# Attention and two feed-forward blocks on one core: the last tile of the spatial product stacked, P V issued ahead of the spread of the inverse sums, dense work given out by rows

## The chip, the cores and the metric

The kernel runs on one core of a Trainium2 chip. Its time is the device time of one execution in microseconds (us), the median of three runs. Where the text speaks of a profiled execution, that is one more execution, recorded instruction by instruction.

## What is computed

Three blocks follow one another on four batches (B = 4) of 576 tokens with 8 heads of 64, so a model width of 512:

```python
scores = scale * q @ k.T                       # per head, 576 x 576
kth = np.partition(scores, -32, axis=-1)[..., -32:-31]
attn = softmax(np.where(scores >= kth, scores, -1e9))
x = attn @ v                                   # heads side by side: B x 576 x 512

xk, xr = mix(x, x_prev, mu_k), mix(x, x_prev, mu_r)
x2 = sigmoid(xr @ w_r) * (relu(xk @ w_k) ** 2 @ w_v)

h = gelu(x2 @ w_in)                            # 1024 columns: u, v
v_n = layernorm(v) * g_ln
v_s = einsum('ts,bsd->btd', w_sg, v_n) + b_sg  # over the 576 tokens
out = x2 + (u * v_s) @ w_out
```

The product with `w_sg`, which runs over the tokens, is called the spatial product here. The weights come as 64-bit floats.

## The kernel before

**Precision.** Products of the dense part work on numbers split into a high and a low part (`split`, line 96: ScalarE copies the high part, GpSimd, or VectorE in the tail, subtracts for the low one). Each product is three passes that add up in PSUM, high by high, low by high and high by low (`PASSES`, line 468: the first index is the part of the activation, the second that of the weight). The weights are converted and split once (`conv`) and kept in scratch in DRAM (`ws_r`, `ws_k`, `ws_v`, `ws_sg`, `ws_h`, `ws_u`, `ws_o`), from which `wload` brings them tile by tile into six buffers `w`.

**Attention.** The work is cut in 80 slots. A slot is 128 rows of queries for two heads (`t.hs` = 2, 256 rows of scores) or, for the last 64 queries of a pair, those of both heads in one tile (`t.hs` = 1, a half slot). Batch 0 goes through its pairs twice, for two slots and then three; the others have five slots for each of four pairs, the fifth a half slot. The slots of one pair that are worked off together are a unit: `u.ch` = 0 has two slots, `u.ch` = 1 has three, the last a half slot. For each slot `emit_S` makes the scores on TensorE, two slots ahead; `emit_topk` finds the 32nd largest value of each row on VectorE (max, match_replace and a last scalar_tensor_tensor that masks the exponentials E and sums them, line 308); `emit_T` transposes E on TensorE into `PT` and, for the 64 last keys, `PTr`. At the end of a unit `emit_unit` (line 337) copies the sums on ScalarE (line 342), inverts them on VectorE (343), spreads them over partitions with small products against the identity (348, and 354 for the half slot; called the spread), copies that to `rb` (357), makes P V in PSUM (`px`; 361 over four tiles of 128 keys, 365 for the last 64), and multiplies both into x (372, 376).

**Dense work.** When a batch's attention is done, `part1` (mixing, lines 499 to 508; the r, k and v products; the product with `w_in`; gelu; layernorm, `norm`) and `part2` (the spatial product `E`, lines 697 to 717, and the output product `F`, 724 to 741) of that batch are cut into items and queued in `Dense`. The loop over the slots runs items until a quota is used up (line 833: the work that is left, divided by the slots up to the next batch); items have a priority five slots later than the slot that gives them out. The part of the last batch runs when all slots are done; this is called the tail.

**Spatial product.** There are eight items `E` for each batch, one for each of four column tiles of v_n and each half (288) of the output tokens. An item sums over five token tiles of v_n: four of 128 rows and one of 64, each in three passes, 15 matmuls in one PSUM bank. Afterwards the result is scaled and biased (711 or 714), multiplied with u and split into `gt`. An item `F` takes 12 matmuls over `gt` and `w_out`.

**Order.** A scheduler orders each engine's instructions by these priorities and by its own estimates. What it makes is fixed: each engine takes its instructions strictly in that order. All DMAs here are issued by SyncE, in order too.

## Time and profile before

| | us |
|---|---|
| median of 3 runs | 1044.78 |
| lowest, highest | 1043.91, 1047.49 |
| profiled execution | 1042.54 |
| its span | 1040.8 |

| engine | busy, us | share of the span |
|---|---|---|
| TensorE matmuls (PE) | 896.8 | 86% |
| TensorE weight loads (PEld) | 766.4 | 74% |
| VectorE (DVE) | 888.0 | 85% |
| ScalarE (ACT) | 716.5 | 69% |
| GpSimd (POOL) | 509.7 | 49% |

In the rows further down, the slices cut the span in 40 pieces of 26 us; each digit is the busy share in tenths. A stage row has the start and end, its length, then for each engine the busy time and the number of instructions, then TensorE's granted clock as a share of full speed, the busy share of the DMA engines and their GB/s. A group row has the line, engine, operation, output and inputs, shapes and count, then the busy time in us and the mean in ns, then the idle time ahead of these instructions and what ended it. A timeline row has the start, the duration, engine, line, operation and count, and in brackets the idle time of that engine just before and its releaser ("issue" is a wait that no recorded event explains). A row of the chain of work that ended last has start, duration, engine, output, line and count. A transfer row ends with the size and the median time from issue to landing. Matmuls overlap, so their durations in a row are longer than their spacing. An fp32 product shows as two records.

### The profile page before, as it was taken

How to read it: one execution, taken by the hardware profiler on the slowest of the kernel's cores; microseconds unless marked ns; L12 is line 12 of the kernel's file. 1: busy time of each engine (PE TensorE's matmuls, PEld its weight loads, DVE VectorE, ACT ScalarE, POOL GpSimd, SP SyncE). 2: the span in 40 equal slices, each digit the busy share in tenths (PEclk: the TensorE clock that was granted, in tenths of full speed). 3: DMA queues.
4: the chain of work that ended last, by engine and by line, in shares of the span. 5: the costliest groups of instructions: out<-in, count | busy, mean ns of one | idle time of the engine just before them, and what ended most of it. 6: DMA issues, size and time to landing. Idle time of an engine off the chain costs nothing.

```text
span 1040.8 us, 18998 instructions
## 1 busy us (share of the span) xinstructions
PE 896.8 (86%) x6158; PEld 766.4 (74%) x6158; DVE 888.0 (85%) x2509; ACT 716.5 (69%) x1591; POOL 509.7 (49%) x624
## 2 busy tenths in 40 slices
PE   3542656689989998977999999998999999999997
PEld 2432444469868987866988887777998888799895
DVE  5999899999989999999999999999999998812142
ACT  6866876877598769666786688667786696554340
POOL 6877676745276317766733217389242135310051
PEclk9965665779989999988999999999999999999999
DMA  7674873567745653541333443254333434765431
GB/s 207 221 256 154 271 254 123 179 229 246 236 174 181 198 176 114 165 159 28 130 112 97 138 120 90 73 173 166 107 130 98 135 87 137 285 240 150 117 98 65
DMA packets 103406, 164.36 MB, mean 158 GB/s; under 512 B 19201, under 2 KB 72961, under 8 KB 103297
## 3 DMA queue, kind: packets, MB, share of 16 engines
q1 hardware_dynamic: 103296, 163.05, 48.4%
q8 instruction: 51, 0.84, 0.3%
q14 instruction: 59, 0.48, 0.1%
HBM read 133.09 MB, written 29.92 MB: 157 GB/s over the span
## 4 chain that ended last, share of the span: by engine, by line
PE 43%; DVE 25%; ACT 9%; POOL 5%; issue 3%; DMA 2%; SPq 0%; DVEq 0%; POOLq 0%; ACTq 0%
PE d L515 7%; PE d L580 7%; DVE M L281 6%; DVE T L287 5%; DVE E L308 5%; PE d L704 4%; PE tp L361 4%; PE d L625 3%; DVE T L273 3%; PE tp L515 2%; PE S L238 2%; DVE T L272 2%; PE d L732 2%; PE tp L321 2%; DVE M L292 2%
## 5 line engine op out<-in xcount | busy, mean ns | idle before, releaser
L281 DVE MAX8 M<-T 128x8 f32<-128x288 f32 x576 | 237.7, 444 | 1.4
L287 DVE MATCH_REPLACE8 T<-M,T 128x288 f32<-128x288 f32 x432 | 187.6, 439 | 0.0
L515 PE MATMUL d<-xm,w 128*128 128x288 f32 (+2 forms) x1008 | 159.6, 308 | 8.6 <-POOL xm L100 4.9
L515 PEld LDWEIGHTS d<-xm,w 128*128 128x128 f32 x1008 | 143.4, 196 | 11.5 <-POOL xm L100 5.8
L238 PE MATMUL S<-kst,qst 128*128 128x288 f32 x512 | 114.5, 342 | 43.1 <-ACT qst L200 26.1
L308 DVE SCALAR_TENSOR_TENSOR E<-S,kth,E 128x576 f32<-128x576 f32 x144 | 146.0, 1045 | 1.4 <-ACT kst L213 0.5
L321 PE MATMUL tp<-ident,E 128*128 128x128 f32 x512 | 87.0, 308 | 48.9 <-ACT kst L207 21.2
L238 PEld LDWEIGHTS S<-kst,qst 128*128 128x128 f32 x512 | 85.0, 213 | 53.3 <-ACT qst L200 27.2
L321 PEld LDWEIGHTS tp<-ident,E 128*128 128x128 f32 x512 | 67.7, 158 | 57.2 <-ACT kst L207 22.2
L307 ACT ACTIVATE E<-S,nb 128x576 f32<-128x576 f32 x144 | 104.9, 770 | 1.2
L580 PE MATMUL d<-ksq,w 128*128 128x288 f32 (+2 forms) x672 | 101.4, 300 | 0.0
L240 ACT ACTIVATE S<-S 128x576 f32<-128x576 f32 x128 | 83.2, 650 | 23.4 <-PE S L238 22.2
L580 PEld LDWEIGHTS d<-ksq,w 128*128 128x128 f32 x672 | 91.6, 188 | 0.7 <-issue 0.6
L322 ACT ACTIVATE PT<-tp 128x512 f32<-128x512 f32 x128 | 73.7, 598 | 19.6 <-PE tp L321 19.4
L273 DVE TENSOR_TENSOR T<-S 128x576 f32<-128x576 f32 (+1 forms) x80 | 81.1, 1014 | 0.0
L272 DVE TENSOR_TENSOR T<-S 128x576 f32<-128x576 f32 (+1 forms) x81 | 69.6, 859 | 9.4 <-ACT S L240 9.3
L704 PE MATMUL d<-w,vn 128*128 128x288 f32 (+1 forms) x420 | 71.8, 310 | 0.5 <-DMA w<-ws_sg 0.5
L361 PE MATMUL tp<-PT,rawv 128*64 128x256 f32 (+1 forms) x512 | 71.7, 424 | 0.0
L100 POOL TENSOR_TENSOR ksq<-tmp,ksq 128x576 fp32r<-128x576 f32 (+2 forms) x32 | 40.3, 1260 | 54.3 <-ACT ksq L98 54.2
L704 PEld LDWEIGHTS d<-w,vn 128*128 128x128 f32 (+1 forms) x420 | 58.4, 187 | 10.0 <-issue 7.8
L100 POOL TENSOR_TENSOR splk<-rawk,splk 128x256 fp32r<-128x256 f32 x40 | 33.2, 831 | 62.5 <-ACT splk L98 52.7
L292 DVE MAX8 M<-T 128x8 f32<-128x288 f32 x144 | 58.5, 440 | 0.0
(162 smaller groups left out, 2010.5 us busy)
## 6 DMA issues: line engine op xcount, KB each, us to landing
w<-ws_k SPq DMA_DIRECT2D x40, 512.0 KB, 4.2
w<-ws_v SPq DMA_DIRECT2D x40, 512.0 KB, 4.4
w<-ws_r SPq DMA_DIRECT2D x20, 512.0 KB, 4.6
w<-ws_h SPq DMA_DIRECT2D x20, 512.0 KB, 3.8
w<-ws_u SPq DMA_DIRECT2D x20, 512.0 KB, 4.1
w<-ws_sg SPq DMA_DIRECT2D x32, 288.0 KB, 3.3
w<-ws_o SPq DMA_DIRECT2D x16, 512.0 KB, 4.8
rawk<-in_k_dram SPq DMA_DIRECT2D x40, 128.0 KB, 3.0
```

What stands on the lines that cost most here:

```text
L238: nc.tensor.matmul(ps[:, hf, :HALF], lhsT=su.qst[h, t.u.ch][:, a, 128 * t.i:128 * t.i + 128], rhs=su.kst[h][:, HALF * hf:HALF * hf + HALF] ...
L272: nc.vector.tensor_tensor(T[:, h, :HALF], t.S[:, h, :HALF], t.S[:, h, HALF:], op=OP.max)
L273: nc.vector.tensor_tensor(T[:, :, HALF:], t.S[:, :, :HALF], t.S[:, :, HALF:], op=OP.min)
L281: nc.vector.max(M[:, h, 8 * r:8 * r + 8], src[h])
L287: nc.vector.match_replace(L[h], M[:, h, 8 * r:8 * r + 8], src[h], NEG)
L307: nc.scalar.activation(E, Sx, AF.Exp, bias=nb[:, h:h + 1], scale=0.125)
L308: nc.vector.scalar_tensor_tensor(E, Sx, kv[h], E, op0=OP.is_ge, op1=OP.mult, accum_out=u.sums[:, c + h:c + h + 1])
L321: nc.tensor.transpose(ps[:, kc, :], E[:, h, 64 * h + 128 * kc:64 * h + 128 * kc + 128], ident)
L361: nc.tensor.matmul(px[64 * h:64 * h + 64, :n], lhsT=vr[:, 4 * h + kc, :], rhs=u.PT[h][:, kc, :n], start=(kc == 0), stop=False)
L515: nc.tensor.matmul(ps[:, :n_], lhsT=w[:, bb, 128 * c:128 * c + 128], rhs=act[ch, which, c][:, a, o:o + n_], start=(c == 0 and i == 0), sto ...
L580: nc.tensor.matmul(ps[:, :nn], lhsT=w[:, bb, 128 * (f % 4):128 * (f % 4) + 128], rhs=kt[f][:, a, o:o + nn], start=(f == 0 and i == 0), sto ...
L704: nc.tensor.matmul(ps[:, :HALF], lhsT=act[b, "vn", i][:nn, a, 128 * m:128 * m + 128], rhs=W["sg", i, si][:nn, bb, :HALF], start=(j == 0), ...
```

## The change

Three edits.

The last token tile of v_n has 64 rows. The change puts its low part into partitions 64 to 127 of the tile's high part (a DMA from SBUF to SBUF behind the split, in `norm`) and keeps the weights of that tile with their high part twice, one above the other, and their low part above zeros (`conv`). One pass of 128 rows then gives high by high plus low by high, and a second gives high by low: an item of the spatial product has 14 matmuls, all of 128 rows. The loads of these weights now bring 128 rows.

In `emit_unit` the P V products over the four full key tiles are written ahead of the spread, and the products over the last 64 keys behind it, alternating with the spread of the half slot; the copy to `rb` comes after both.

The quota of a slot is weighed by its rows (`t.hs`) against the rows of the slots up to the next batch, instead of by the number of slots.

```diff
@@ -341,6 +341,11 @@
         rinv = sb.tile([128, 5], F32, tag="rinv", name="rinv", bufs=2)
         nc.scalar.activation(rinv[:, :nt], u.sums[:, :nt], AF.Copy, bias=1e-9)
         nc.vector.reciprocal(rinv[:, :nt], rinv[:, :nt])
+        px = bank("tp")
+        for kc in range(4):
+            for h in range(2):
+                nc.tensor.matmul(px[64 * h:64 * h + 64, :n], lhsT=vr[:, 4 * h + kc, :], rhs=u.PT[h][:, kc, :n],
+                                 start=(kc == 0), stop=False)
 
         ps = bank("tp")
         for i in range(2):
@@ -348,21 +353,14 @@
                 nc.tensor.matmul(ps[64 * h:64 * h + 64, 128 * i:128 * i + 128],
                                  lhsT=rinv[:, 2 * i + h:2 * i + h + 1].to_broadcast([128, 64]), rhs=ident,
                                  start=True, stop=True)
-        if u.ch:
-            for h in range(2):
-                s = slice(64 * h, 64 * h + 64)
+        for h in range(2):
+            s = slice(64 * h, 64 * h + 64)
+            nc.tensor.matmul(px[s, :n], lhsT=vr[s, 8, :], rhs=u.PTr[s, :n], start=False, stop=True)
+            if u.ch:
                 nc.tensor.matmul(ps[s, 256:320], lhsT=rinv[s, 4:5].to_broadcast([64, 64]), rhs=ident[s, s],
                                  start=True, stop=True)
         rb = sb.tile([128, 320], F32, tag="rb", name="rb", bufs=1)
         nc.scalar.activation(rb[:, :n], ps[:, :n], AF.Copy)
-        px = bank("tp")
-        for kc in range(4):
-            for h in range(2):
-                nc.tensor.matmul(px[64 * h:64 * h + 64, :n], lhsT=vr[:, 4 * h + kc, :], rhs=u.PT[h][:, kc, :n],
-                                 start=(kc == 0), stop=False)
-        for h in range(2):
-            s = slice(64 * h, 64 * h + 64)
-            nc.tensor.matmul(px[s, :n], lhsT=vr[s, 8, :], rhs=u.PTr[s, :n], start=False, stop=True)
         if (b, p) not in xT:
             x = sb.tile([128, S + 1], F32, tag="x", name="x", bufs=5)
             xT[b, p] = x
@@ -424,6 +422,11 @@
                 split(w[:n, 0, :HALF], w[:n, 1, :HALF], nat[:n, HALF * hf:HALF * hf + HALF])
                 scr = dram.tile([128, 2, HALF], F32, name=f"ws_sg{i}_{hf}")
                 nc.sync.dma_start(scr[:n], w[:n, :, :HALF].bitcast(F32))
+                if n == 64:
+
+                    nc.gpsimd.memset(w[64:, 1, :HALF].bitcast(F32), 0.0)
+                    nc.sync.dma_start(scr[64:, 0], w[:64, 0, :HALF].bitcast(F32))
+                    nc.sync.dma_start(scr[64:, 1], w[64:, 1, :HALF].bitcast(F32))
                 wscr["sg", i, hf] = scr
             return
         H, L = raw[:, :, 1], raw[:, :, 0]
@@ -459,9 +462,8 @@
             tag = WTAGS[wturn[0] % len(WTAGS)]
             wturn[0] += 1
         w = sb.tile([128, 2, 512], F32R, tag=tag, name="w", bufs=WBUFS[tag])
-        n = 64 if key[:2] == ("sg", 4) else 128
-        wv = w[:n, :, :HALF] if kind == "sg" else w
-        nc.sync.dma_start(wv.bitcast(F32), wscr[key][:n])
+        wv = w[:, :, :HALF] if kind == "sg" else w
+        nc.sync.dma_start(wv.bitcast(F32), wscr[key])
         return w
 
 
@@ -645,6 +647,9 @@
             nc.gpsimd.tensor_scalar(ag[:nn, 3:4], ag[:nn, 0:1], -1.0, 1.0, op0=OP.mult, op1=OP.mult)
             nc.gpsimd.tensor_scalar(t, y, ag[:nn, 3:4], ag[:nn, 2:3], op0=OP.add, op1=OP.mult)
             split(a[:nn, 0], a[:nn, 1], t)
+            if nn < 128:
+
+                nc.sync.dma_start(a[64:, 0].bitcast(F32), a[:64, 1].bitcast(F32))
             if len(segs) == 2 or i > 1:
                 act[b, "vn", i] = a
             else:
@@ -699,10 +704,9 @@
             ps = bank("d")
             j = 0
             for i in range(5):
-                nn = 128 if i < 4 else 64
-                for a, bb in PASSES:
-                    nc.tensor.matmul(ps[:, :HALF], lhsT=act[b, "vn", i][:nn, a, 128 * m:128 * m + 128],
-                                     rhs=W["sg", i, si][:nn, bb, :HALF], start=(j == 0), stop=(j == 14))
+                for a, bb in (PASSES if i < 4 else ((0, 0), (0, 1))):
+                    nc.tensor.matmul(ps[:, :HALF], lhsT=act[b, "vn", i][:, a, 128 * m:128 * m + 128],
+                                     rhs=W["sg", i, si][:, bb, :HALF], start=(j == 0), stop=(j == 13))
                     j += 1
             y = tmp()[:, :HALF]
             if si == 0:
@@ -830,7 +834,7 @@
         if s in ready:
             ready[s]()
         nxt = min([r for r in ready if r > s], default=NS)
-        quota = 0.995 * dense.left() / (nxt - s)
+        quota = 0.995 * dense.left() * t.hs / sum(x.hs for x in slots[s:nxt])
         with at(1000 * (s + 5) + 500):
             while dense.items and quota > 0:
                 quota -= dense.run()
```

How this moves instructions. On TensorE at the end of the last slot, where E_11596 (before) and E_11581 (after) are the masked exponentials of the last, half slot, tp and d are PSUM banks, L732 (L736) is the output product of batch 2 and L704 the spatial product, before:

```order
L704 MATMUL d<-w,vn 128x288 x16
L732 MATMUL d<-w,gt 128x512 x6
L329 MATMUL tp<-ident,E_11596 128x128 x4
L333 MATMUL tp<-ident,E_11596 64x64
L334 MATMUL tp<-ident,E_11596 64x64
L732 MATMUL d<-w,gt 128x512 x3
L348 MATMUL tp<-ident,rinv 64x128 x4
L354 MATMUL tp<-ident,rinv 64x64 x2
L732 MATMUL d<-w,gt 128x512 x9
L361 MATMUL tp<-PT,rawv 64x320 x8
L365 MATMUL tp<-PTr,rawv 64x320 x2
L732 MATMUL d<-w,gt 128x512 x18
```

and after, at the same place:

```order
L736 MATMUL d<-w,gt 128x512 x18
L329 MATMUL tp<-ident,E_11581 128x128 x4
L333 MATMUL tp<-ident,E_11581 64x64
L334 MATMUL tp<-ident,E_11581 64x64
L736 MATMUL d<-w,gt 128x512 x18
L347 MATMUL tp<-PT,rawv 64x320 x8
L353 MATMUL tp<-ident,rinv 64x128 x4
L358 MATMUL tp<-PTr,rawv 64x320
L360 MATMUL tp<-ident,rinv 64x64
L358 MATMUL tp<-PTr,rawv 64x320
L360 MATMUL tp<-ident,rinv 64x64
L736 MATMUL d<-w,gt 128x512 x12
```

Twelve more output matmuls stand ahead of the last slot's transposes, the spread has moved behind P V, and 24 output matmuls follow the unit (the 12 shown and 12 of 64 rows).

On TensorE in the tail, at the start of the last batch's spatial product (vn_12678 before and vn_12663 after are the last token tile, the numbers of d and tp tell the items apart), before:

```order
L704 MATMUL tp_12744<-w_12470,vn_12678 128x288
L704 MATMUL d_12766<-w_12394,vn_12596 128x288 x2
L704 MATMUL d_12766<-w_12422,vn_12624 128x288 x3
L704 MATMUL tp_12744<-w_12470,vn_12678 128x288 x2
L704 MATMUL d_12766<-w_12468,vn_12650 128x288 x3
L704 MATMUL d_12766<-w_12470,vn_12678 128x288 x3
```

and after:

```order
L708 MATMUL d_12751<-w_12453,vn_12635 128x288 x3
L708 MATMUL tp_12772<-w_12333,vn_12555 128x288 x3
L708 MATMUL tp_12772<-w_12379,vn_12581 128x288 x3
L708 MATMUL tp_12772<-w_12407,vn_12609 128x288 x3
L708 MATMUL tp_12772<-w_12453,vn_12635 128x288 x3
L708 MATMUL tp_12730<-w_12455,vn_12663 128x288 x2
L708 MATMUL d_12751<-w_12455,vn_12663 128x288 x2
L708 MATMUL tp_12772<-w_12455,vn_12663 128x288 x2
```

The last tile's matmuls of the first item stood among those of the second; now the full tiles of three items come first, 36 matmuls, and then the last tile of all three.

On VectorE at the end of the top-k part (L714 and L718 are the bias step of the spatial product, L504 and L506 a mix of the next batch, L308 the last step of the last slot), before:

```order
L714 SCALAR_TENSOR_TENSOR tmp_11293<-d_11277,gln_77,bsg_78 128x288
L281 MAX M_11469<-T2_11594 128x8
L295 TENSOR_REDUCE M_11469<-M_11469 128x8
L296 TENSOR_REDUCE kth_11470<-M_11469 128x1
L308 SCALAR_TENSOR_TENSOR E2_11596,sums_11468<-S2_11455,kth_11470,E2_11596 128x576
L714 SCALAR_TENSOR_TENSOR tmp_11314<-d_11298,gln_77,bsg_78 128x288
L504 SCALAR_TENSOR_TENSOR tmp_11671<-x_9191,omu_76,tmp_11671 128x576
```

and after:

```order
L718 SCALAR_TENSOR_TENSOR tmp_11299<-d_11284,gln_77,bsg_78 128x288
L287 MATCH_REPLACE T2_11579<-M_11454,T2_11579 128x288
L281 MAX M_11454<-T2_11579 128x8
L295 TENSOR_REDUCE M_11454<-M_11454 128x8
L296 TENSOR_REDUCE kth_11455<-M_11454 128x1
L506 SCALAR_TENSOR_TENSOR tmp_11656<-x_9168,omu_76,tmp_11656 128x576
L308 SCALAR_TENSOR_TENSOR E2_11581,sums_11453<-S2_11440,kth_11455,E2_11581 128x576
```

The bias step of the batch's last item and one mix have moved ahead of the last top-k step.

## Rows read from the trace of the kernel before

**Rows 1.** Page, 40 equal slices of the span, busy tenths

```profile
PE   3542656689989998977999999998999999999997
...
DVE  5999899999989999999999999999999998812142
```

**Rows 2.** Stages: PE, PEld, DVE, ACT, POOL busy (count), clock, DMA

```profile
400.00:500.00 100.00, 86.30 (x561) 70.94 (x560) 97.74 (x272) 71.85 (x157) 70.51 (x72) 0.91 0.35 113
...
700.00:800.00 100.00, 96.25 (x750) 87.09 (x749) 98.38 (x296) 74.54 (x171) 50.02 (x53) 0.98 0.39 127
...
889.94:1000.57 110.63, 110.63 (x754) 101.58 (x752) 37.25 (x71) 54.56 (x115) 16.28 (x31) 1.00 0.62 202
1000.57:1019.94 19.37, 19.37 (x124) 16.44 (x122) 7.76 (x15) 6.20 (x14) 7.36 (x8) 1.00 0.01 3
```

**Rows 3.** Groups of VectorE instructions between 300 and 890 us

```profile
L714 DVE SCALAR_TENSOR_TENSOR tmp<-d,gln,bsg 128x288 f32<-128x288 f32 x16 | 8.0, 506 | 3.2 <-PE d L704 3.2
L343 DVE RECIPROCAL rinv<-rinv 128x5 f32<-128x5 f32 (+1 forms) x22 | 3.8, 171 | 9.9 <-ACT rinv L342 9.9
```

**Rows 4.** Timeline around the last slot's end, all engines

```profile
888.54 1.38 DVE L308 SCALAR_TENSOR_TENSOR E<-S,kth,E 128x576 f32<-128x576 f32 x1
...
890.29 0.80 DVE L504 SCALAR_TENSOR_TENSOR tmp<-x,omu,tmp 128x576 f32<-128x576 f32 x1
...
894.32 0.42 ACT L357 ACTIVATE rb<-tp 128x320 f32<-128x320 f32 x1
...
898.09 0.19 PEld L365 LDWEIGHTS tp<-PTr,rawv 64*64 64x64 f32 x4 [0.49 <-issue]
...
898.78 3.95 PEld L732 LDWEIGHTS d<-w,gt 128*128 128x128 f32 x18 [0.49 <-issue]
...
898.90 0.42 DVE L372 TENSOR_TENSOR x<-tp,rb 128x256 f32<-128x256 f32 x1 [2.46 <-PE tp L365]
...
902.99 1.23 PE L515 MATMUL tp<-xm,w 128*128 128x288 f32 x8
```

**Rows 5.** Chain of work that ended last, two of its pieces

```profile
943.64 1.58 PE d L515 x12
...
1022.96 2.75 PE d L732 x12
```

**Rows 6.** Timeline of weight loads, one spatial item in the tail

```profile
1010.44 1.61 PEld L704 LDWEIGHTS tp<-w,vn 128*128 128x128 f32 x12 [0.16 <-issue]
1012.22 0.42 PEld L704 LDWEIGHTS tp<-w,vn 64*128 64x128 f32 x3 [0.16 <-issue]
1012.82 1.62 PEld L704 LDWEIGHTS d<-w,vn 128*128 128x128 f32 x12 [0.17 <-ACT gt L98]
```

**Rows 7.** Timeline at the start of the tail's spatial product

```profile
1000.70 1.48 PE L704 MATMUL tp<-w,vn 128*128 128x288 f32 x10
...
1002.64 0.68 DVE L100 TENSOR_TENSOR vn<-tmp,vn 64x512 fp32r<-64x512 f32 x1 [1.18 <-ACT vn L98]
```

**Rows 8.** Transfers of 128 KB: count, size, median us to landing

```profile
rawv<-in_v_dram SPq DMA_DIRECT2D x40, 128.0 KB, 2.3
...
x2sTrue<-xn SPq DMA_DIRECT2D x8, 128.0 KB, 3.0
...
out_dram<-xr SPq DMA_DIRECT2D x4, 128.0 KB, 4.0
```

**Rows 9.** Group of GpSimd instructions, forms kept apart

```profile
L100 POOL TENSOR_TENSOR w<-nat,w 128x288 fp32r<-128x288 f32 x8 | 8.0, 1008 | 1.4 <-ACT w L98 1.4
```

**Rows 10.** Groups of ScalarE table loads, forms kept apart

```profile
L480 ACT ACT_TABLE_LOAD x15 | 19.2, 1283 | 0.3
...
L307 ACT ACT_TABLE_LOAD x14 | 18.0, 1283 | 0.3
```

**Rows 11.** Stages of line 308 on VectorE alone

```profile
400.00:500.00 100.00, 21.78 (x36) 0.91 0.35 113
...
700.00:800.00 100.00, 19.20 (x36) 0.98 0.39 127
```

## Prediction

> **What bounds the kernel now.** I read the slices of the whole span first [rows 1]: VectorE is at eight or nine tenths from the second slice up to about 860 us, and at one to four tenths after about 910 us, where TensorE stays at nine. So there are two parts with different limits. In the stages [rows 2] the top-k part shows VectorE busy 97.74 and 98.38 of 100 us; TensorE is close behind it, but VectorE is the engine that hardly ever waits. From 889.94 to 1019.94 TensorE is busy every microsecond (110.63 of 110.63, then 19.37 of 19.37), at the full granted clock of 1.00, which is the 2.4 GHz level, while VectorE is busy for about a third of the time. The turn between the two parts is the last top-k instruction of the last slot, at 888.54 [rows 4].
>
> This sorts the edits. A TensorE microsecond saved behind the turn is a microsecond of the end. One saved ahead of it counts only where VectorE waits for it. In the list of VectorE groups between 300 and 890 us [rows 3] those waits are few: 9.9 us for the copy of the row sums on ScalarE and 3.2 us for the spatial product are the largest.
>
> **Part 1, the stacked last tile.** Each item of the spatial product takes 15 matmuls: 12 of full height and 3 of 64 rows. The loads show what the short tile costs [rows 6]: 12 loads take 1.61 us, then stand 0.16 us, 3 short loads take 0.42 us, and another 0.17 us passes before the next item; start to start that is 2.38 us. Twelve matmuls of the same 288 columns without a change of height take 1.58 us [rows 5], 0.132 us each, and there the result changes from item to item as well, so the gaps belong to the change of height. Fourteen full matmuls should take 14 x 0.132 = 1.85 us, 0.53 us less. The tail has eight items, which took 19.37 us [rows 2]; 112 matmuls at 0.132 us are 14.8 us, a gain of **4.5 us**. The other 24 items lie in the top-k part and save about as much each, but VectorE hides them.
>
> The Trainium skill ("TensorE: Matmul & The Clock Gate", section "LDWEIGHTS (loading the stationary operand)") says that a load's time follows its columns and not its rows. The rows agree for the load alone (0.42 us for 3, 1.61 us for 12), but they show two gaps more, which that rule doesn't have; by the rule alone the tail's gain would be 8 x 0.132 = 1.1 us.
>
> What it adds: a copy from SBUF to SBUF of 128 KB for each batch, behind the split of the last tile, which the last two matmuls of an item wait for. In the tail the split ends at 1002.64 + 0.68 = 1003.32 [rows 7]. No such copy is in the trace; transfers of 128 KB land between 2.3 and 4.0 us after their issue, those of the same size that start in SBUF and go to a scratch in 3.0 us [rows 8]; so it lands between 1005.6 and 1007.3. By the order, 36 matmuls of three items now stand ahead of the first that needs it: 1000.70 + 36 x 0.132 = 1005.5. TensorE waits between 0.1 and 1.8 us; I take **+0.8 us**, by the 3.0 us, since that transfer too starts in SBUF. Behind it on its queue stand only result stores and reloads of x, which are not wanted before 1020. In the other three batches the copy stands ahead of the second half of the spatial weights on SyncE's queue; a late copy there holds TensorE, and so the scores for a later slot, but these are given out two slots ahead (some 20 us). I cost it at nothing; without that cover it is 3 x 3.0 us. The padded stores and two clears happen once, in the first 200 us; a GpSimd pass over 288 columns takes 1.0 us [rows 9], so they are 2 us on GpSimd at most and nothing on the path.
>
> **Part 2, P V ahead of the spread.** The number of matmuls is the same. In units with a half slot the two 64-row spreads now stand among the 64-row products, so two turns of height become one pair. Such a turn shows 0.49 us on either side of the last products [rows 4]. For the last unit I count **-0.3 us** (bounds 0 and -1.0); the other 15 such units lie under VectorE. The price: the copy of the spread (rb, 0.42 us on ScalarE at 894.32 [rows 4]) ran beside P V before; now it comes behind the unit's last matmul, and x follows it. In the last unit x is then some 1.3 us later than 898.90. That is covered: from x to the first product that needs it took about 4.1 us (898.90 to 902.99 [rows 4]), and by the order 24 matmuls of the output product (24 x 0.23 = 5.5 us, 2.75 us for 12 [rows 5]) and at least nine others now stand there.
>
> **Part 3, dense work by rows.** It changes nothing in the total; I counted the dense matmuls between the transposes of one slot and the next in the order of either kernel. The half slots don't get less: work is given out five slots ahead, and TensorE runs late, so it lands anywhere. What does change is the end: before the last slot's transposes 18 output matmuls now stand instead of 6 (60 in the batch). Those 12 leave the tail: 12 x 0.23 = **-2.75 us**. They cost nothing where they go, since the eight spatial items of this batch just before give back 8 x 0.53 = 4.2 us. On VectorE, however, a bias step (0.5 us) and a mix (0.8 us, as at 890.29) now stand ahead of the last top-k step, and three bias steps in a row wait for items whose matmuls are interleaved. Against that stand the 3.2 us of such waits of before [rows 3], which shrink with the items. The bounds are -2 and +1.3 us; I take **+0.5 us**.
>
> **The top-k part as a whole.** All orders shift, and VectorE's own instructions stay the same in number. ScalarE loses four of its 29 table loads (1.28 us each [rows 10]), and the 9.9 us in which VectorE waited for the copy of the sums stand partly behind such loads. On the other side, the same 36 score steps took 21.78 us in one stage and 19.20 us in another [rows 11], the longer with GpSimd busy 70.51 us and the shorter with 50.02 us [rows 2]: a new neighbourhood can stretch or shorten VectorE by 2 or 3 us in 100 us, mostly cancelling over eight such stages. I take **-1.0 us**, with bounds -6 and +4.
>
> **Sum**, against the profiled execution (1042.54 us, span 1040.8): -4.5 + 0.8 - 0.3 - 2.75 + 0.5 - 1.0 = -7.25, so 1035.3 us. The median of the runs is 2.2 us above the profiled one; carried over, the forecast is 1044.8 - 7.25 = **1037.5 us**.
>
> **Rivals.** (a) The gaps belong to something else, say the turn from one item to the next, and stay; then the stacked tile gives 8 x 0.132 = 1.1 us and not 4.5: 1040.9 us. For it: the second gap does stand at a turn. Against: the first doesn't, and plain items turn without one [rows 5]. This is also what the skill's rule on loads named above would give. Chance 0.10.
> (b) TensorE is nearer to being the bound of the top-k part than VectorE's busy share tells, and the 12.7 us that 24 items save there, with fewer table loads, take away 5 us of the 9.9 + 3.2 us of waits beyond what I counted: 1032.5 us. Chance 0.13.
> (c) The new order puts more GpSimd passes beside VectorE's score steps or makes it wait in-order for dense results, 4 us in all over 890 us: 1041.5 us. Chance 0.12.
> (d) Slower: x now waits for a copy that starts only behind the unit's last product. VectorE takes its work in order, so if the two multiplies of a unit stand too early, it idles in each of 31 units for the copy (0.42 us) and whatever ScalarE has in hand (0.6 us or so). It needs 0.34 us a unit, 10.5 us in all, to bring the kernel to 0.3% slower; 0.45 us a unit gives 1051 us. Against it: the rows show no such wait among the large ones between 300 and 890 us, and the order keeps some 15 VectorE instructions between the reciprocal and the multiplies. Chance 0.07.
>
> **How the numbers follow.** The forecast has 0.58. About 0.3% (3.1 us) is what a measurement of this kernel can tell from no change. Faster by more: nearly all of the forecast (0.56), all of (b), 0.06 of (a) and half of (c), 0.81, which I round to 0.80. Slower by more: most of (d), 0.06. The rest, 0.14, is no change. The range takes in (a), (c) and most of (b): 1031.0 to 1043.5 us.
>
> **What would show it.** In the profile after: items of 14 matmuls at 1.85 us, no 64-row loads in the spatial product, the tail from the last top-k step to the end shorter by some 7 us, one wait of 0.1 to 1.8 us for the copy about three items into the last spatial product, 25 table loads for gelu and exp in place of 29, and the last top-k step within 2 us of 888.5. It is wrong if that step moves by more than 4 us, if VectorE waits for x in many units, or if items still take over 2 us.

## The result and the profile after

| | before | after |
|---|---|---|
| median of 6 runs each, us | 1044.35 | 1029.96 |
| lowest, highest | 1042.97, 1047.49 | 1026.84, 1033.3 |
| profiled execution | 1042.54 | 1030.12 |
| its span | 1040.8 | 1027.9 |
| start of the span to the end of the last top-k step | 889.9 | 882.8 |
| from there to the end | 150.9 | 145.1 |

The ratio is 0.987 (95% interval 0.9847 to 0.9893); the medians are 14.4 us apart, where 7.25 were forecast. 1029.96 lies 1 us under the range. Of the 12.9 us between the spans, 7.0 lie ahead of the last top-k step and 5.9 behind it; the forecast had 0.5 and 6.75. The tail came out about as long as worked out. The top-k part did not.

The slices of the page after, to set beside [rows 1], show the same two parts:

```profile
PE   3652656679989998977999998999999998999996
...
DVE  5999899999999989899999989899999989722142
```

Stages of before (first two lines) and of after (last two), from 260 us to the last top-k step and from there to the end; columns as in [rows 2]:

```profile
260.00:889.86 629.86, 596.73 (x4291) 514.13 (x4290) 598.60 (x1780) 464.68 (x1019) 304.37 (x371) 0.98 0.42 134
889.94:1040.80 150.86, 144.12 (x935) 128.63 (x933) 50.13 (x96) 61.20 (x129) 24.54 (x40) 0.99 0.49 160
```

```profile
260.00:882.82 622.82, 586.02 (x4258) 513.84 (x4258) 592.11 (x1770) 459.81 (x1015) 307.65 (x371) 0.98 0.43 138
882.90:1027.90 145.00, 136.97 (x917) 125.33 (x915) 48.35 (x94) 58.66 (x126) 22.12 (x38) 0.99 0.51 162
```

The first line of before is what the prediction should have printed. Over the whole stretch TensorE is busy 596.73 of 629.86 us and VectorE 598.60: both 95%, each idle for 31 to 33 us. The two stages of [rows 2] had shown 86 and 96 us of 100 for TensorE, and the text called VectorE alone the bound. After the change TensorE has 10.7 us less work in this stretch and VectorE 6.5 us less, though VectorE has 2509 instructions in either kernel. Part of that comes from where the window begins: the last top-k step of batch 0 ends at 262.5 us before and at 259.4 after, so 10 instructions fewer lie in the second window. From that step to the last one the time is 627.5 and 623.4 us. VectorE's busy time in it falls from 596.2 to 592.7 us, and 3.1 of these 3.5 us are in line 308; its idle time falls from 31.3 to 30.7 us. So of the 7.0 us about 3 lie in batch 0, which the prediction did not look at, 3.5 are shorter VectorE instructions, and only 0.6 are shorter waits.

The tail's spatial product in the chain of work of after (start, duration, engine, output, line, count):

```profile
994.19 1.58 PE tp L708 x12
995.77 0.13 issue
995.89 0.50 PE tp L708 x2
996.39 0.26 PE d L708 x2
996.66 0.26 PE tp L708 x2
996.92 1.84 PE d L708 x14
998.77 1.84 PE tp L708 x14
```

and the copy on its queue and the first loads that need it, in the timeline:

```profile
993.49 0.52 SPq L652 DMA_DIRECT2D vn<-vn  x1
...
995.86 0.30 PEld L708 LDWEIGHTS tp<-w,vn 128*128 128x128 f32 x2 [0.33 <-issue]
```

Fourteen matmuls take 1.84 us (forecast 1.85; 2.38 for the 15 of [rows 6]); the copy landed 2.3 us after its issue and was used 2.4 us after it, and TensorE stood 0.33 us for it.

The last slot's end in the timeline of after, to set beside [rows 4]:

```profile
881.53 1.35 DVE L308 SCALAR_TENSOR_TENSOR E<-S,kth,E 128x576 f32<-128x576 f32 x1
...
882.00 2.35 PE L736 MATMUL d<-w,gt 128*128 128x512 f32 x9 [0.99 <-DMA w<-ws_o]
...
884.19 0.60 PE L329 MATMUL tp<-ident,E 128*128 128x128 f32 x4
...
893.14 0.44 ACT L363 ACTIVATE rb<-tp 128x320 f32<-128x320 f32 x1 [6.77 <-PE tp L360]
893.62 0.43 DVE L370 TENSOR_TENSOR x<-tp,rb 128x256 f32<-128x256 f32 x1 [3.35 <-ACT rb L363]
```

Of the 18 output matmuls ahead of the last transposes, nine waited for their weights and ran while the last top-k step was ending; five of them began behind its end. The output product's share of the tail, before (first line) and after, with the busy time and the number of its matmuls and then of its weight loads:

```profile
889.94:1040.80 150.86, 28.50 (x119) 20.26 (x117) 0.99 0.49 160
882.90:1027.90 145.00, 25.68 (x109) 18.47 (x107) 0.99 0.51 162
```

Ten output matmuls have left the tail, 2.8 us of busy time, where the forecast had 12 and 2.75 us.

VectorE's waits of after between 260 and 883 us (us in total, times, longest), beside [rows 3]:

```profile
DVE rinv L343 <- ACT rinv L342: 11.0, 6, 4.0
DVE bst L643 <- ACT vraw L482: 5.1, 3, 3.8
DVE tmp L718 <- PE d L708: 4.0, 3, 2.1
DVE T L272 <- ACT S L240: 2.3, 2, 2.1
DVE x L370 <- ACT rb L363: 1.7, 2, 1.2
```

The wait of x for the copy rb, the mechanism of rival (d), is 1.7 us in two places. The wait for the sums (9.9 us in [rows 3], 11.0 here) did not shrink.

### The profile page after: what moved, and what is told of

Its sections match the earlier page's. It is cut to its first block, busy times and chain, and to the rows that moved or that the text cites. A ratio compares the mean times of both kernels' runs of the same rounds, so it can differ in the third digit from the quotient of the medians.

```text
span 1027.9 us, 18922 instructions
## 1 busy us (share of the span) xinstructions
PE 880.5 (86%) x6126; PEld 767.2 (75%) x6126; DVE 882.6 (86%) x2509; ACT 712.3 (69%) x1587; POOL 514.3 (50%) x626
## 4 chain that ended last, share of the span: by engine, by line
PE 42%; DVE 35%; ACT 10%; POOL 6%; issue 3%; DMA 3%; SPq 1%; DVEq 0%; POOLq 0%; ACTq 0%
DVE M L281 9%; PE d L582 8%; DVE T L287 8%; PE d L517 7%; DVE E L308 6%; PE d L627 4%; DVE T L273 3%; DVE T L272 3%; PE S L238 3%; PE tp L347 3%; PE tp L517 2%; PE d L736 2%; DVE M L292 2%; PE tp L321 2%; PE d L708 2%
## 5 line engine op out<-in xcount | busy, mean ns | idle before, releaser
L281 DVE MAX8 M<-T 128x8 f32<-128x288 f32 x576 | 237.8, 444 | 1.5
L517 PE MATMUL d<-xm,w 128*128 128x288 f32 (+2 forms) x1008 | 154.5, 303 | 8.0 <-DMA w<-ws_k 3.3
L517 PEld LDWEIGHTS d<-xm,w 128*128 128x128 f32 x1008 | 140.6, 192 | 9.9 <-DMA w<-ws_k 3.4
L308 DVE SCALAR_TENSOR_TENSOR E<-S,kth,E 128x576 f32<-128x576 f32 x144 | 143.6, 1028 | 1.1 <-ACT E L307 0.5
L321 PEld LDWEIGHTS tp<-ident,E 128*128 128x128 f32 x512 | 64.7, 156 | 66.1 <-ACT kst L207 26.6
L240 ACT ACTIVATE S<-S 128x576 f32<-128x576 f32 x128 | 83.5, 652 | 19.5 <-PE S L238 18.1
L347 PE MATMUL tp<-PT,rawv 128*64 128x256 f32 (+1 forms) x512 | 83.3, 445 | 1.2 <-ACT PT L322 1.1
L708 PE MATMUL d<-w,vn 128*128 128x288 f32 x392 | 62.4, 309 | 2.8 <-DMA w<-ws_sg 1.7
L347 PEld LDWEIGHTS tp<-PT,rawv 128*64 128x64 f32 x512 | 42.0, 148 | 28.9 <-issue 6.5
L708 PEld LDWEIGHTS d<-w,vn 128*128 128x128 f32 x392 | 56.2, 197 | 5.2 <-DMA w<-ws_sg 2.1
```

Source lines behind the costliest of these rows:

```text
L281: nc.vector.max(M[:, h, 8 * r:8 * r + 8], src[h])
L308: nc.vector.scalar_tensor_tensor(E, Sx, kv[h], E, op0=OP.is_ge, op1=OP.mult, accum_out=u.sums[:, c + h:c + h + 1])
L321: nc.tensor.transpose(ps[:, kc, :], E[:, h, 64 * h + 128 * kc:64 * h + 128 * kc + 128], ident)
L347: nc.tensor.matmul(px[64 * h:64 * h + 64, :n], lhsT=vr[:, 4 * h + kc, :], rhs=u.PT[h][:, kc, :n], start=(kc == 0), stop=False)
L517: nc.tensor.matmul(ps[:, :n_], lhsT=w[:, bb, 128 * c:128 * c + 128], rhs=act[ch, which, c][:, a, o:o + n_], start=(c == 0 and i == 0), sto ...
L708: nc.tensor.matmul(ps[:, :HALF], lhsT=act[b, "vn", i][:, a, 128 * m:128 * m + 128], rhs=W["sg", i, si][:, bb, :HALF], start=(j == 0), stop ...
```

## Experiments

Ratios are to the kernel before, measured beside each kernel, with 95% intervals; "ends" is when the last top-k step ends, "tail" the rest of the span, both of the profiled execution. Profiled executions of one kernel differ by a few us, so the ratios decide and the two columns only tell where.

| kernel | ratio | ends | tail |
|---|---|---|---|
| stack alone | 0.9938 (0.9917 to 0.9958) | 892.8 | 147.2 |
| P V order alone | 0.9942 (0.9926 to 0.9959) | 886.4 | 148.0 |
| quota by rows alone | 0.9965 (0.9945 to 0.9986) | 881.1 | 156.7 |
| P V + rows, no stack | 0.9998 (0.9978 to 1.0018) | 891.5 | 149.4 |
| stack + rows, P V as before | 0.9908 (0.9875 to 0.9941) | 884.3 | 147.2 |
| stack + P V, old quota | 0.9787 (0.9752 to 0.9822) | 875.0 | 147.2 |
| all three (the change) | 0.9870 (0.9847 to 0.9893) | 882.8 | 145.1 |
| stack in batches 0 to 2 only | 0.9940 (0.9923 to 0.9956) | 883.6 | 148.5 |
| stack in batch 3 only | 0.9922 (0.9905 to 0.9938) | 885.2 | 146.8 |
| the change, +4 matmuls an item | 0.9933 (0.9917 to 0.9950) | 880.9 | 153.6 |
| the change, +12 matmuls an item | 1.0071 (1.0053 to 1.0088) | 878.4 | 169.4 |
| stack + P V ahead, turns not merged | 0.9837 (0.9804 to 0.9869) | 879.4 | 145.1 |
| stack + turns merged, spread first | 0.9895 (0.9874 to 0.9915) | 889.9 | 137.5 |

**One edit at a time.** The stack alone (the diff of `conv`, `wload`, `norm` and `E`):

> Before with the stacked tile alone (14 full-height matmuls an item, copy and padded weights). By the order, 18 output matmuls stand ahead of the last slot's transposes here too, against 6 of before. Theory R (relief: TensorE's lighter items are what shortens the top-k part): the last top-k step ends 5 to 7 us earlier than before, the tail is 5 to 6 us shorter, 1031 to 1034 us in all. Theory W (weights: the quota by rows is what shortens the top-k part): only the tail gains, 1038 to 1040 us. Theory O (any new order moves the top-k part by several us, whatever the edit): anything between 1031 and 1043 us, not adding up with the other edits.

The P V order alone (the diff of `emit_unit`):

> Before with P V ahead of the spread alone. By the order, 18 output matmuls ahead of the last transposes too. Theory R: TensorE loses only some turns of height (half a us for each of 16 units), so the top-k part gains at most 2 us and the tail 2 to 3 us by the moved output matmuls: 1040 to 1042 us. Theory W: the same. Theory O: 1036 to 1047 us, with a top-k part that moves by several us although TensorE's work is nearly the same.

The quota by rows alone:

```diff
-        quota = 0.995 * dense.left() / (nxt - s)
+        quota = 0.995 * dense.left() * t.hs / sum(x.hs for x in slots[s:nxt])
```

> Before with the quota by rows alone. By the order, no output matmul stands ahead of the last transposes, 6 fewer than before (1.4 us more in the tail). Theory W: the top-k part ends 5 to 7 us earlier, 1038 to 1041 us in all. Theory R: the top-k part stays within 1 us, 1045 to 1046 us. Theory O: 1040 to 1050 us.

Each alone is faster than before, by 6.5, 6.1 and 3.6 us (by the ratios; the medians, which the expectations further down use, are 6.5, 7.1 and 4.1 us apart). With the quota alone the top-k part ends 9 us earlier but the tail is 6 us longer: none of the 60 output matmuls of batch 2 stand ahead of the last transposes, against 6 before and 18 with either of the other edits. So the matmuls that left the tail were not moved by the quota.

**One edit undone.** These are the changed kernel with the old `emit_unit`, with the old spatial product, and with the old quota (the diffs above, reversed):

> The changed kernel with the spread ahead of P V as before (stacked tile and quota by rows). Theory A: 6.5 + 4.1 us less than before, 1033 to 1035 us. Theory O: anything from 1030 to 1040 us.

> The changed kernel without the stacked tile (P V order and quota by rows). Theory A: 7.1 + 4.1 us less than before, 1033 to 1035 us. Theory R, that TensorE's lighter items carry most of it: 1039 us or more. Theory O: anything from 1030 to 1042 us.

> The changed kernel with the old quota (stacked tile and P V order together). Alone they gave 6.5 and 7.1 us, the quota by rows 4.1 us; all three gave 14.4 us. Theory A (each edit has its own gain, and they add up but for a few us): 1030 to 1032 us, as fast as the changed kernel or nearly, so the quota is worth under 2 us on top. Theory O (each number is what its own order happens to cost in the top-k part): 1030 to 1040 us, unrelated to the sum. Theory W, that the quota is needed for the gain: 1036 us or more.

The edits don't add up. Taken over the four pairs with and without it, the stack gives -0.0062, -0.0155, -0.0057 and -0.0128 (mean -0.0100, 10.5 us), the P V order -0.0058, -0.0151, +0.0033 and -0.0038 (mean -0.0054), and the quota -0.0035, +0.0056, -0.0030 and +0.0083 (mean +0.0018). Without the quota by rows the kernel is faster than the changed one: 1022.82 us.

**How much is the order's luck?** The factor 0.995 of the quota was changed, which leaves all work as it is and was meant to put dense items elsewhere. Of the kernel before and of the changed kernel:

> Control: before with the factor of the quota at 0.97 in place of 0.995. No work is changed, but the order differs in many places; 6 output matmuls ahead of the last transposes, as before. Theories R and W: within 2 us of before, 1043 to 1046 us. Theory O: it may differ by several us, since a new order alone moves the top-k part.

> Control: the changed kernel with the factor of the quota at 0.97. No work is changed; the order differs in many places, with the same 18 output matmuls ahead of the last transposes. Theory A: within 2 us of the changed kernel, 1028 to 1032 us. Theory O: 1026 to 1038 us.

> Control: the changed kernel with the factor 0.98 in place of 0.995, a third order of its work. If the quota by rows itself costs some 9 us: 0.986 to 0.992 of before, as the changed kernel (0.987) and its control with 0.97 (0.991). If the old quota's three orders were only luckier: any value down to 0.978.

> The same with the factor 1.0, a fourth order. As for the run before: 0.986 to 0.992 if the quota by rows costs by itself, down to 0.978 if it is luck.

and of the version with the stack and the P V order under the old quota:

> Control: stack and P V order with the old quota, its factor 0.97 in place of 0.995. The work is the same, dense items fall elsewhere. If 1022.8 us is the level of this version: within 4 us of it, 0.975 to 0.983. If it was a lucky order and the quota by rows costs nothing as such: at the level of the changed kernel and of its control, 1030 to 1034 us, 0.987 to 0.991.

> The same control with the factor 1.03: a third order of the same work. As for the run before: 0.975 to 0.983 if the old quota is better by itself, 0.987 to 0.991 if it is not.

Before: 1.0001 (0.9984 to 1.0017). Changed kernel: 0.9913 (0.9884 to 0.9941), 0.9887 (0.9830 to 0.9944) and 0.9867 (0.9811 to 0.9923), with its own 0.9870 a mean of 0.9884 over the four. Old quota: 0.9785 (0.9763 to 0.9806) and 0.9770 (0.9751 to 0.9790), with 0.9787 a mean of 0.9781 over the three. So on top of the other two edits the kernels with the quota by rows are some 10 us slower than those with the old one. Luck is not excluded by this, though, since the factor moved next to nothing. In the traces VectorE's 2509 instructions, compared by operation and tile, stand in the same order as with 0.995 but for 2 in the kernel before, 11, 9 and none in the changed kernel (0.97, 0.98, 1.0), and 2 and none with the old quota (0.97, 1.03). With 1.0 the other compute engines keep their order too, so that run is a repeat of the changed kernel. Undoing the quota in the changed kernel moves 138 of them, and from before to after 184 have moved. So the controls show that the two levels stand, not that other orders of the same work would stand on them; whether the quota itself or its one order costs the 10 us is open. The factor 1.03 gives the lowest median of this study, 1020.52 us.

Where the 10 us go can be read in the traces in part. From the end of the first batch's last slot to the last top-k step the three with the old quota take 613.5 to 614.9 us, the four with the new one 622.6 to 626.6; the tails are alike (144.9 to 147.2 and 144.7 to 146.7). In that stretch it is VectorE's last top-k step, line 308, that differs most. All of its 144 runs in the span, with their min, median and max in ns, in the changed kernel:

```profile
L308 DVE SCALAR_TENSOR_TENSOR E<-S,kth,E x144: 790/817/2209, 28.2 to 881.5; 128x576 f32<-128x576 f32 x144
```

in the version with the old quota:

```profile
L308 DVE SCALAR_TENSOR_TENSOR E<-S,kth,E x144: 791/810/1978, 27.8 to 873.7; 128x576 f32<-128x576 f32 x144
```

The same instruction takes 0.8 us mostly and over 2 us at times; the sum over all 144 is 146.0 us before, 140.9 to 144.9 in the four kernels with the quota by rows and 135.0 to 136.5 in the three with the old quota. Two places in the timeline of the changed kernel tell when, the first without GpSimd, the second with two steps beside it:

```profile
267.58 0.80 DVE L308 SCALAR_TENSOR_TENSOR E<-S,kth,E 128x576 f32<-128x576 f32 x1
...
457.89 1.40 POOL L509 TENSOR_TENSOR tmp<-tmp 128x576 f32<-128x576 f32 x1
458.48 1.42 DVE L308 SCALAR_TENSOR_TENSOR E<-S,kth,E 128x576 f32<-128x576 f32 x1
...
459.25 1.92 POOL L100 TENSOR_TENSOR xm<-tmp,xm 128x576 fp32r<-128x576 f32 x1
...
459.84 1.95 DVE L308 SCALAR_TENSOR_TENSOR E<-S,kth,E 128x576 f32<-128x576 f32 x1
...
460.06 0.81 PE L321 MATMUL tp<-ident,E 128*128 128x128 f32 x4 [4.17 <-DVE E L308]
```

I set each single record of line 308 from 260 us on beside GpSimd's. Those with no GpSimd instruction beside them take 0.79 to 0.83 us in every kernel. Those with one: 54 of 109 before, 1.26 us on average; 65 of 108 in the changed kernel, 1.14 us; 55 of 109 with the old quota, 1.06 us. The last of the rows above shows what follows: TensorE stood 4.17 us at the transposes of the first of the two E, whose step took 1.42 us in place of 0.80, so 0.6 us of that wait is the stretching. In all the transposes of full slots (line 321) waited 4.7 to 8.7 us for line 308 between 260 and 880 us in the four kernels with the quota by rows, 2.2 us in the three with the old one.

So with the quota by rows GpSimd's passes stretch the last top-k steps by some 7.5 us more (the means of the two groups of sums). That is not yet most of the 10 us. In the stretch from batch 0 to the last top-k step all of VectorE's busy time is 592.0 to 595.3 us in the four and 588.4 to 588.7 in the three, some 5 us apart, and its idle time 30.6 to 33.0 against 25.0 to 26.2, some 6 us apart. TensorE's granted clock there is 0.970 to 0.984 in the four and 0.986 to 0.989 in the three, so the clock may have a share as well. Nor does the sum of line 308 go with the time elsewhere: it is 140.9 us without the stack (ratio 0.9998) and 148.2 us with the stack alone (0.9938), against 146.0 before. No run took GpSimd's passes away, so their share of the 10 us is not shown.

The Trainium skill ("SBUF — State Buffer", section "SBUF: two separate sides") says that VectorE and GpSimd share a pair of ports, that a VectorE instruction with two inputs in SBUF and a GpSimd instruction that reads SBUF lock each other out of it, and that the loser waits for the whole of the other's instruction. Line 308 has two such inputs. The trace agrees roughly: the record of 1.95 us above began beside a GpSimd pass and ended 0.62 us behind it, where 0.80 would be due had it waited for all of it, and 18 of the 65 records beside a GpSimd instruction in the changed kernel are no longer than those alone.

**Does TensorE's time count in the top-k part?** Theory T says it does, rival V that VectorE hides it, as the prediction had it. First the stack in some batches only, on the changed kernel (the main lines, here for the tail alone; the other has `b < B - 1`):

```diff
-            if nn < 128:
+            if nn < 128 and b == B - 1:
...
+            stk = b == B - 1
             for i in range(5):
-                for a, bb in (PASSES if i < 4 else ((0, 0), (0, 1))):
+                nn = 128 if i < 4 or stk else 64
+                for a, bb in (PASSES if i < 4 or not stk else ((0, 0), (0, 1))):
```

> The changed kernel, but the last token tile is stacked in batches 0 to 2 only; the tail keeps items of 15 matmuls. Theory T (TensorE's time in the top-k part counts: it sits just behind VectorE, and what 24 items give back there shortens that part): only the tail's 4.5 us are lost against the changed kernel, 1030 + 4.5 = 1034.5 us, 0.9905 of before. Rival V (VectorE hides TensorE there, as the prediction had it; what the singles gave beyond the tail is the chance of the new order): nothing is gained by these 24 items, so about the time without the stack, 1043 us, 0.999, give or take 4 us for the order.

> The changed kernel, but stacked in the last batch only, which lies in the tail. Theory T: without the stack 1043.2 us was measured; the tail gives back 4.5 us: 1038.7 us, 0.9945 of before, and the last top-k step stands some 8 us later than in the changed kernel. Rival V: the whole gain of the stack that is not the order's is here, so the top-k part ends where it ended in the changed kernel, within 4 us: 1030 us, 0.986.

Both lie between the theories. Against 0.9998 without the stack, the tail's eight items give 0.0076 and the other 24 give 0.0058 (6.0 us); together 0.0134, where the whole stack gives 0.0128. But with the stack in the tail only, 6.3 us lie ahead of the last top-k step, where no item is stacked (891.5 to 885.2 us): VectorE has the same work there, and 101 of its 2509 instructions have moved. I put that down to the order. So an order alone can be worth about 6 us (one profiled execution of each; two of nearly the same order of before end 2.5 us apart), and these two runs decide nothing on the 24 items. For the tail they do: the kernel with the stack in batches 0 to 2 has the changed kernel's order on VectorE but for one instruction, is 0.0070 slower (7.3 us, give or take 3), and its profiled span is 4.2 us longer; the forecast's 4.5 us for the tail's items fits both.

Then the reverse, as a dose: matmuls that are overwritten, ahead of each item of batches 0 to 2 (with 12 in place of 4 in the second):

```diff
+            for q in range(4 if b < B - 1 else 0):
+                nc.tensor.matmul(ps[:, :HALF], lhsT=act[b, "vn", q // 3][:, 0, 128 * m:128 * m + 128],
+                                 rhs=W["sg", q // 3, si][:, 0, :HALF], start=True, stop=True)
```

> The changed kernel with four more matmuls ahead of each spatial item of batches 0 to 2, into the item's own bank and overwritten by it: 24 x 4 x 0.132 = 12.7 us more on TensorE, all in the top-k part, nothing else. Theory T: the top-k part gets longer by what the stack had shortened it, some 9 us: 1039 us, 0.9945. Rival V: TensorE's added time is hidden: 1030 us, 0.986, give or take 4 us for the order.

> The same with twelve more matmuls an item: 24 x 12 x 0.132 = 38 us more on TensorE in the top-k part. Theory T: more than two thirds of it shows, 26 to 38 us: 1056 to 1068 us, 1.011 to 1.023 of before. Rival V: VectorE still hides it, up to 5 us: 1030 to 1035 us, at most 0.991. Between them, TensorE's time would count in part and by place.

Against the changed kernel the 12.7 us added cost 0.0063 (6.6 us), and the 38 us cost 0.0201 (21 us): a little over half of what is added shows; against the mean of the four kernels with the quota by rows, 0.40 and 0.51. Neither theory gave that, and T was wrong about where. The top-k part does not get longer, it ends earlier (878.4 us with 38 us more), and the tail takes it all: 169.4 us against 145.1. The order moved here too (107 and 178 of VectorE's instructions), so the smaller dose, 6.6 us, is within what an order can be worth; the 21 us of the larger are not, and rival V, at most 0.991, is wrong. The stages of the kernel with 12 more:

```profile
260.00:878.37 618.37, 597.51 (x4362) 529.16 (x4361) 588.33 (x1760) 453.17 (x1002) 290.49 (x357) 0.98 0.42 133
878.45:1047.80 169.35, 162.16 (x1095) 149.63 (x1093) 53.27 (x102) 63.27 (x136) 33.36 (x52) 0.99 0.49 158
```

and TensorE's timeline there, more than 20 us after the last top-k step (706 are added matmuls, 711 the items, 739 the output product, all of batch 2):

```profile
901.78 1.74 PE L706 MATMUL d<-w,vn 128*128 128x288 f32 x12
903.36 2.00 PE L711 MATMUL d<-w,vn 128*128 128x288 f32 x14
905.21 8.71 PE L739 MATMUL d<-w,gt 128*128 128x512 f32 x36
```

Batch 2's dense work, given out five slots late, slips past the last top-k step when TensorE has no room for it: in this tail TensorE is busy 162.16 us, 25.2 more than in the changed kernel, of the 38 added. There every microsecond counts. That is how TensorE's time in the top-k part reaches the end here although VectorE sets the pace of the slots.

**Why does the P V order help?** Theory W: TensorE has P V to do while the sums are inverted, in place of standing at the spread. Theory H: the merged changes of height. One of each, on the stack with the old quota. P V whole, then the spreads:

```diff
+        for h in range(2):
+            s = slice(64 * h, 64 * h + 64)
+            nc.tensor.matmul(px[s, :n], lhsT=vr[s, 8, :], rhs=u.PTr[s, :n], start=False, stop=True)
         ps = bank("tp")
...
-            nc.tensor.matmul(px[s, :n], lhsT=vr[s, 8, :], rhs=u.PTr[s, :n], start=False, stop=True)
```

> Stack and P V order with the old quota, but all P V products (64-row ones too) stand ahead of all spreads, so units with a half slot keep two changes of height; TensorE still has P V to do while VectorE inverts the sums. Theory W (P V ahead helps because TensorE no longer stands at the spread): the time of the version with the merged turns, 1023 us, 0.979 of before. Theory H (it helps by the merged turns of height): near the stack alone, 1037 us, 0.994. Theory O (what the P V order gave beside the stack is mostly the chance of the order): anywhere between, 1025 to 1035, and the same for the next run.

and the spread first, then its 64-row part, the 64-row P V and the full P V:

```diff
+            nc.tensor.matmul(px[s, :n], lhsT=vr[s, 8, :], rhs=u.PTr[s, :n], start=True, stop=False)
...
-                                 start=(kc == 0), stop=False)
+                                 start=False, stop=(kc == 3))
```

> Stack with the old quota; the spread first as in the kernel before, but the 64-row spreads and the 64-row P V products side by side (one change of height and back), the full P V products last. Theory W: as the stack alone, 1037 us, 0.994. Theory H: 1023 us, 0.979. Theory O: between, within 5 us of the run before this one.

From the stack alone (0.9938) W gives 0.0101 (10.5 us) and H 0.0043 (4.5 us); the two together give 0.0157 (to 0.9781). So, in these orders, P V ahead of the spread gave twice as much as the merged turns. That is one order for each of the first two, and some 150 of VectorE's instructions moved against the stack alone, so theory O is not excluded. Theory W's reason can be looked for in the groups of weight loads between 260 and 880 us, where the last columns are idle time ahead of them. The stack alone:

```profile
L361 PEld LDWEIGHTS tp<-PT,rawv 128*64 128x64 f32 x384 | 27.0, 142 | 18.1 <-issue 3.2 <-ACT PT L322 0.3 <-ACT u L671 0.2
L348 PEld LDWEIGHTS tp<-ident,rinv 128*64 128x64 f32 x192 | 10.6, 142 | 10.5 <-ACT PT L322 7.7 <-issue 0.9 <-DVE T L287 0.5
L365 PEld LDWEIGHTS tp<-PTr,rawv 64*64 64x64 f32 x96 | 4.7, 131 | 11.1 <-issue 7.1 <-ACT E L307 1.9 <-ACT PTr L325 1.3
```

stack and P V order, old quota:

```profile
L347 PEld LDWEIGHTS tp<-PT,rawv 128*64 128x64 f32 x384 | 27.9, 138 | 22.0 <-issue 3.9 <-ACT PT L322 1.4 <-ACT u L669 0.5
L353 PEld LDWEIGHTS tp<-ident,rinv 128*64 128x64 f32 x192 | 16.4, 137 | 3.9 <-DVE T L287 0.2 <-issue 0.2
L358 PEld LDWEIGHTS tp<-PTr,rawv 64*64 64x64 f32 x96 | 4.7, 131 | 5.0 <-issue 3.6 <-ACT PTr L325 1.2 <-ACT E L307 0.2
```

The idle time at the spread falls from 10.5 to 3.9 us, and at the 64-row products from 11.1 to 5.0, 3.5 us of that "issue". But most of the wait at the spread was ended by ScalarE's copies of PT (7.7 us), which P V needs too, and none of it by the inverse (line 343); and ahead of the full P V products the idle time rises from 18.1 to 22.0 us. With the 64-row spread (2.2 and 2.9 us) the four groups stand 41.9 us with the stack alone and 33.8 us with both. W's own version stands 44.9 us and is 10 us faster than the stack alone, and the kernel before stands 34.3 us. So theory W's version was faster, but not for theory W's reason as far as these waits show.

What does go with the gain is line 308: its sum is 148.2 us with the stack alone, 141.2 in H's version, 136.3 in W's and 135.0 with both. So the new orders may have helped by taking GpSimd's passes off VectorE's steps, a rival that no run separates from W and H. With the quota by rows the same edit gave little either way (+0.0033 without the stack, -0.0038 with it), and there that sum hardly moved (142.5 to 140.9 us, 143.6 to 143.6).

## Why the prediction was wrong

**Part 1 in the tail** was right: 1.84 us an item against 1.85, so 4.3 of the 4.5 us. Rival (a), 1.1 us, is out: the two gaps went with the short tile. The wait for the copy was 0.33 us (0.8 taken, bounds 0.1 and 1.8).

**The top-k part as a whole** is the term of the sum that failed: -1.0 taken, bounds -6 and +4, and the last top-k step came 7.0 us earlier. By the prediction's own sign (more than 4 us) that makes it wrong. It had counted on new neighbourhoods "mostly cancelling". In their place stand about 3 us in batch 0, which it had not looked at, 3.5 us of VectorE's busy time, of which line 308 alone is 3.1, and 0.6 us of waits. Which edit brought these about is open: each version with an edit undone has another order, and an order alone was worth about 6 us once.

**Part 1 in the top-k part** has the step of the reasoning that failed: "The other 24 items lie in the top-k part and save about as much each, but VectorE hides them." Putting 38 us of TensorE's time back there cost 21 us, a little over half, as batch 2's dense work slipped past the last top-k step. For the 12.7 us that the 24 items save themselves, 6.0 us (stack in batches 0 to 2) and 6.6 us (the smaller dose) were measured, no more than an order can be worth. Rival (b) had named this and had priced it at 5 us (chance 0.13); its mechanism was off, since VectorE's waits hardly shrank.

**Part 2** was mis-sized the same way. It counted the last unit (-0.3 us) and laid the other units under VectorE. On the stack with the old quota the order is worth 16 us; with the quota by rows it gained 4 us with the stack and lost 3 without. Why is not shown: TensorE's waits in the units do not account for it, and line 308 grew shorter by 13 us along with it.

**Part 3** had the tail's number about right and its cause and the sign of the whole wrong. Ten output matmuls left the tail (12 forecast). But the 18 that stand ahead of the last transposes stand there with the stack alone or the P V order alone too, and none with the quota alone. The changed kernel is 0.0083 (8.7 us) slower than the version with the old quota. Rival (c), that the new order puts GpSimd's passes beside VectorE's steps (4 us), fits a part of that loss; against the kernel before, line 308 grew shorter by 3.1 us, not longer.

**Rival (d)** did not happen: x waited 1.7 us for rb.

In the order stack, P V, quota the edits measured -6.5, -15.8 and +8.7 us, which is the ratio 0.987. The sum had -3.7 (-4.5 + 0.8), -0.3 and -2.25 (-2.75 + 0.5), and -1.0 for all that moves. That the time lies only 1 us under the range is luck: a gain and a loss that the sum had not seen stand against each other.

## What to carry to other kernels

Read the busy shares over the whole stretch that sets the end, not in two windows: where two engines are both at 95%, do not set the work of the one that "is not the bound" to nothing. Here half of what was added to it reached the end, as later work that slipped behind the stretch. Where a scheduler decides the order, undo each edit alone and shake the order before a gain is put down to an edit, and look in the trace whether the shake moved anything: the factor used here hardly did. The version with one of the three edits undone was the fastest. When VectorE is the pace, look at which GpSimd passes stand beside its instructions with two inputs.

## What the runs showed of the hardware

The VectorE step of line 308 (128 x 576, two inputs in SBUF) takes 0.79 to 0.83 us alone. Beside a GpSimd instruction it takes 1.06 to 1.26 us on average from 260 us on, at most 2.25 us in the kernel before. The longest of all runs, 3.91 us in the kernel with the stack in batches 0 to 2, stands at 146 us beside several GpSimd passes in a row. I had known a stretch of two or three us in 100 from [rows 11]; that it sits in single records, each beside a GpSimd instruction, I had not.

An item of 12 matmuls of 128 rows and 3 of 64 took 2.38 us, one of 14 of 128 rows 1.84 us. Of these 0.54 us the one matmul saved is 0.13 us; the other 0.4 us went with the change to 64-row weights and back. The copies of 128 KB from SBUF to SBUF landed 2.3 us after their issue, at the lower end of the 2.3 to 4.0 us of [rows 8].
